# Attention and expert layer in one kernel: the first twelve score tiles in cycles of two slots, and attention products in the gaps between score tiles

## The chip, the cores and the metric

One core of one Trainium2 chip runs the whole program. The metric is the device time of one execution in microseconds (us); the time of the kernel before is the median of three runs.

## The reference

Attention with a threshold, and then a feed-forward layer with a hard-swish gate on its output. There are 8 batches, 8 heads, 576 rows and a head dimension of 64.

```python
scores = scale * np.matmul(q, k.transpose(0, 1, 3, 2))
thresh = np.max(scores, axis=-1, keepdims=True) - tau
scores = np.where(scores >= thresh, scores, -1000000000.0)
attn = np.exp(scores - np.max(scores, axis=-1, keepdims=True))
attn = attn / (np.sum(attn, axis=-1, keepdims=True) + 1e-09)
x = matmul(attn, v), with the heads side by side    # 4608 x 512
h = x @ w_in                                        # 512 -> 2048
out = (h * np.clip(h + 3.0, 0.0, 6.0) / 6.0) @ w_out
```

## The kernel before

**Slots.** The attention is cut into 144 slots (`queue`, lines 188 to 195), 18 for each batch. A slot is 128 rows of q for two heads, so it has two score tiles of 128x576. On every slot the same steps run, each on its own engine:

- TensorE (PE) multiplies q by k into PSUM, in float32, with a contraction of 32 rows at a time. `scores` (line 233) does one slot; `burst` (line 208) does two slots, an even one and the odd one after it, interleaved, so that four groups of 32 rows of the array are in use instead of two.
- VectorE (DVE) copies each tile out of PSUM and takes its row maximum on the way: `sm_max`, line 265, two instructions per slot. `sm_recip` (line 287) later inverts the row sums.
- GpSimd (POOL) makes a bias from the maximum (line 274) and later scales the tile into bf16 (`sm_norm`, line 292).
- ScalarE (ACT) applies the threshold (`sm_mask`, line 279) and the exponential (`sm_exp`, line 284).
- The scaled tile is transposed, by a DMA issued from SyncE (line 303) or, for the slots marked `on_chip`, by PE and a DVE copy (`pe_transpose`, lines 305 to 310).
- PE multiplies the transposed tiles by v (`av`, line 317); DVE copies the product into `xT` (`av_main`, line 325) or `xR` (`av_rest`, line 334). Below these are called **products**.

**The expert layer.** When the four products of a batch and chunk are there, eight items of the first expert matmul are put on the list `todo1` (`whole`, line 408), and four more for every two batches (`odd_items`). Each slot from slot 11 on takes one item: `mm1`, then a relu on ACT (odd slots, line 358) or DVE (even slots, line 360), then the gate on DVE (line 373). Parts of the second expert matmul (`mm2_part`) are done two at a time in odd slots (`second`, line 486). What is left when the 144 slots are done is worked off in a tail (`rest1`, `rest2`, `last_tile`).

**PSUM.** It has eight banks of 512 float32 columns. `score_col` (line 201) puts the score tiles of an even slot at columns 896 to 1472 (banks 1 and 2) and those of an odd slot at 64 to 640 (banks 0 and 1); the second tile of each lies three banks further (banks 4 and 5, and 3 and 4). Bank 1, and bank 4, is thus shared by an even and an odd slot. Banks 6 and 7 (`HB`, `OB`) serve the expert matmuls, the PE transposes and, ahead of slot 11, the products. From slot 11 on the products go to `bank()` (line 178), which is the start of bank 2 or bank 5 in turn, that is, a place in the even slot's own banks.

**Order.** The order of each engine is written by hand: the loop at line 497 emits, for slot n, the maxima of slot n+1, the reciprocal of slot n-1, waiting copies, scores of slot n+2 (while n is at most N1 = 11), the products, an mm1 item, PE transposes, mm2 parts, the exponentials of slot n, the thresholds of slot n+1, transposes of q and k (`jobs`), the scaling of slot n-1, and from slot 12 on, in even slots, the burst of slots n+2 and n+3. Every engine works its list off strictly in that order; what one engine needs of another is a semaphore wait that the recording layer adds. `products`, `jobs`, `issues` and `v_pieces` (lines 420 to 473) say in which slot each product, transpose and load stands.

Of the kernel before, what the change touches and what calls it, by code (L numbers as in the profile page):

```python
# [15 lines left out]
P = 128  # L16
# [4 lines left out]
def kernel(  # L21
# [10 lines left out]
    nc = tc.nc  # L32
# [3 lines left out]
    NPAIR = H // 2  # L36
    KI = d_model // P
    NI = d_ff // P
    NSLOT = 18
    N1 = 11  # L40
    HB, OB = 6, 7
    R, T = 32, S // 32
    scale = 1.0 / math.sqrt(D)
# [24 lines left out]
    qkT = {}  # L68
# [7 lines left out]
    def at(when, n, job):  # L76
        when.setdefault(n, []).append(job)
# [70 lines left out]
                            in_=moe_w_out.rearrange("(ni p) f -> p ni f", p=P)[:, 4 * i:4 * i + 4, :])  # L148

    load(0, 1, 0, 10, by=nc.scalar)  # L150
    load(0, 0, 0, 4)
    load(0, 1, 10, T, by=nc.scalar)
    load(1, 1, by=nc.scalar)
    load(0, 0, 4, T)
    load(1, 0)

    identf = singles.tile([P, P], F32)
# [1 line left out]

    def warm_up(count):  # L160
        for _ in range(count):
            nc.tensor.transpose(ps[:, HB, 0:P], identf[:], identf[:])

    blank = nc.const_aps.tensor(0.0, [P, P], F32)
    for _ in range(2):
        nc.tensor.matmul(ps[:, HB, 0:P], blank, blank, start=True, stop=True)
    warm_up(24)
    identb = singles.tile([P, P], BF16)
    nc.vector.tensor_copy(out=identb[:], in_=identf[:])
# [8 lines left out]
    def bank():  # L178
        nonlocal turn
        turn += 1  # L180
        return ps[:, (2, 5)[turn % 2], :]

    class Slot:
        pass
# [4 lines left out]
    for b in range(B):  # L189
        for g, t in ((0, 0), (0, 1), (1, 0), (1, 1), (None, 4), (0, 2), (0, 3), (1, 2), (1, 3)):  # L190
            for i in range(2):
                sl = Slot()
                sl.b, sl.g, sl.t, sl.i, sl.n = b, g, t, i, len(queue)
                sl.on_chip = sl.n in (1, 3, 5, 6, 7, 8)
                queue.append(sl)


# [3 lines left out]
    def score_col(n, a):  # L201
        return (512 - OWN if n % 2 else 1024 - P) + 1536 * a
# [5 lines left out]
    def burst(n):  # L208
        steps = ((0, 0, P, 0), (1, 0, OWN, 0), (0, 0, P, 1), None,
                 (0, P, OWN, 0), (1, 0, OWN, 1), (0, P, OWN, 1), (1, OWN, P, 0), (1, OWN, P, 1))  # L210
        for step in steps:
# [6 lines left out]
            for a in range(2):  # L218
                c = 32 * (2 * i + a)
                c0 = score_col(n + i, a) + k0  # L220
                for quad, rows, q0 in (((2 * sl.b + sl.g, slice(0, P), sl.t * P),) if sl.t < 4 else
# [4 lines left out]
                                          kT[c:c + 32, j, k0:k0 + w], start=(j == 0), stop=(j == 1))  # L226
                    if (i, k0) == (1, OWN):
                        behind(mm, relay)


    gate = [None]

    def scores(n):
        sl = queue[n]
        quads = [(2 * sl.b + sl.g, slice(0, P), sl.t * P)] if sl.t < 4 else [
            (2 * sl.b + g, slice(64 * g, 64 * g + 64), 512) for g in range(2)]
        own = (P, OWN) if n % 2 == 0 else (0, OWN)
        shared = (0, P) if n % 2 == 0 else (OWN, P)
        for k0, w in (own, shared):
            for j in range(2):  # L240
                for a in range(2):
                    c = 32 * (2 * (n % 2) + a)
                    c0 = score_col(n, a) + k0
                    for quad, rows, q0 in quads:
                        qT, kT = qkT[quad]
                        mm = nc.tensor.matmul(ps_flat[rows, c0:c0 + w],  # L246
                                              qT[c:c + 32, j, q0:q0 + rows.stop - rows.start],
                                              kT[c:c + 32, j, k0:k0 + w], start=(j == 0), stop=(j == 1))
                        if (k0, w) == shared and gate[0] is not None:
                            behind(mm, gate[0])  # L250
        sl.last_mm = mm

    def pass_on(n):
        gate[0] = nc.vector.nop()
        behind(gate[0], queue[n].last_mm)

    def sm_max(sl):
        sl.s = s_pool.tile([P, 2, S], F32, tag="s", name="s")
# [61 lines left out]
    def av_main(b, hp, chunk):  # L320
        if hp == chunk == 0:
            xT[b] = x_pool.tile([P, KI, 512], BF16, tag="xT", name="xT")
        pb = ps[:, OB, P:P + 256] if now < N1 else bank()[:, 0:256]
        av(pb, b, hp, pts[b, hp, chunk], slice(0, 256))
        nc.vector.tensor_copy(out=xT[b][:, hp, 256 * chunk:256 * chunk + 256], in_=pb)  # L325

    def av_rest(b):
        pb = bank()
        for hp in range(NPAIR):
            av(pb[:, 64 * hp:64 * hp + 64], b, hp, ptr[b, hp % 2], slice(64 * (hp // 2), 64 * (hp // 2) + 64))  # L330
        if b % 2 == 0:
            xR[b // 2] = x_pool.tile([P, KI, P], BF16, tag="xR", name="xR")
        o0 = 64 * (b % 2)
        nc.vector.tensor_copy(out=xR[b // 2][:, :, o0:o0 + 64],
                              in_=pb[:, 0:256].rearrange("p (a b) -> p a b", a=NPAIR))

    def half_columns(out, lhsT, rhs, start, stop):
        w = 64 if now < len(queue) - 1 else P
# [82 lines left out]
    for b in range(B):  # L421
        n0 = b * NSLOT
        for hp in range(NPAIR):
            at(products, n0 + 6 + 2 * hp if b else (6, 7, 9, 10)[hp], (b, hp, 0))
            at(products, n0 + 16 + 2 * hp, (b, hp, 1))
        at(products, n0 + 14, (b, None, None))

    def multiply(n):
        for b, hp, chunk in products.get(n, ()):
            if hp is None:  # L430
                av_rest(b)
                if b % 2:
                    todo1.extend(odd_items(b, (0,) if b < B - 1 else (0, 1)))
                elif b:
                    todo1.extend(odd_items(b - 1, (1,)))
            else:
                av_main(b, hp, chunk)
                if hp == NPAIR - 1:
                    todo1.extend(whole(b, chunk))


    for quad in range(2, 2 * B):
        b, g = divmod(quad, 2)
        n0 = (b - 1) * NSLOT
        when = (((6, 7), (9, 10))[g] if b == 1 else ((-2, -1), (6, 7))[g])
        for n, of in zip(when, (1, 0)):
            at(issues, n0 + n, lambda quad=quad, of=of: load(quad, of))
        when = (7, 9, 11, 13) if quad == 2 else ((4, 6, 8, 10), (12, 14, 16, 18))[g]
# [3 lines left out]
    for n, job in ((0, lambda: transpose_k(1, 0)), (0, lambda: transpose_k(1, 1)), (1, lambda: transpose_q(1, 0, 8)),  # L452
                   (2, lambda: transpose_q(0, 8, T)), (4, lambda: transpose_q(1, 8, T))):
        at(jobs, n, job)

# [8 lines left out]
        for i, n in enumerate(slots):  # L464
            at(issues, n, lambda i=i: piece(i))

    v_pieces(0, (0, 0, 1, 1, 2, 2, 3, 3))
    for b in range(1, B):
        v_pieces(b, (16, 17, 18, 19, 20, 21, 22, 23) if b == 1 else [(b - 1) * NSLOT + n for n in range(6, 22, 2)])
    for i, n in enumerate((4, 5, 7, 9)):  # L470
        at(issues, n, lambda i=i: load_w_in(i))
    for i, n in enumerate((11, 13, 15, 17)):
        at(issues, n, lambda i=i: load_w_out(i))

    transpose_k(0, 0)
    transpose_k(0, 1)
    transpose_q(0, 0, 4)
    scores(0)
    pass_on(0)
    sm_max(queue[0])  # L480
    scores(1)
    transpose_q(0, 4, 8)
    for i in range(2):
        sm_mask(queue[0], i)

# [4 lines left out]
            bb, mt, part = todo2.pop(0)  # L490
            mm2_part(mt, part)

    prev = None
    pieces = bb = mt = part = 0
    waiting = []
    outs = []
    for n, sl in enumerate(queue):
        now = n
        if n <= N1:
            pass_on(n + 1)  # L500
        if n + 1 < len(queue):
            sm_max(queue[n + 1])
        if prev is not None:
            sm_recip(prev)
        for copy in waiting:
            copy()
        waiting = []
        if n <= N1:
            scores(n + 2)
        multiply(n)  # L510
        item = None
        if todo1 and n >= N1:
            item, then = todo1.pop(0)
            h = mm1(item, 0 if n == len(queue) - 1 else OB if n > N1 and n % 2 == 0 and not pieces else HB)
# [5 lines left out]
        if n > 1 and queue[n - 2].on_chip:  # L520
            waiting.append(pe_transpose(queue[n - 2]))
# [11 lines left out]
        if prev is not None:  # L533
            sm_norm(prev)
        if n > N1 and n % 2 == 0 and n + 2 < len(queue):
            burst(n + 2)
        if n < 2:
            warm_up(6)
        flush()
        for issue in issues.get(n, ()):  # L540
            issue()
        prev = sl

    for tile in outs:
        late.extend(mm2_out(*tile, on_act=False))
# [11 lines left out]
            by.dma_start(out=out[r0:r0 + P, columns], in_=osb[:, 0:c])  # L557

    def rest1(item, then, on_act=True):
        h = mm1(item, hb=(0, 1, 3, 4)[count[0] % 4])  # L560
        count[0] += 1
        mm1_gate(item, h, mm1_relu(h, on_act))
        todo2.extend(then)
# [12 lines left out]
                late.extend(mm2_out(bb, mt, on_act=(count[1] % 2 == 0)))  # L576
                count[1] += 1

    sm_recip(prev)
    sm_norm(prev)  # L580
    for item in todo1:
        rest1(*item)
    todo1.clear()
    rest2()
    for n in range(len(queue), len(queue) + 5):
        multiply(n)
    for item in todo1:
        rest1(*item)
    rest2()
# [35 lines left out]
```

## Time and profile before

| | us |
|---|---|
| median of 3 runs (lowest, highest) | 558.24 (557.84, 560.10) |
| the profiled execution | 558.5 |
| its span, first to last instruction | 556.7 |
| outside the span | 1.8 |
| PE busy in the span | 524.0 (94%) |
| DVE, ACT, POOL busy | 445.2, 441.8, 280.8 |
| mean granted TensorE clock | 0.926 |
| end of the maxima of slot 13 | 82.8 |

The page of a profile gives the busy time of each engine, then the span in 40 slices of 13.9 us in which each digit is a share in tenths: of busy time, and for PEclk of the full TensorE clock. A busy PE is not a PE at its peak: at half clock the same matmuls are simply busy for longer. The timeline lists instructions in order of time, with start and length in us, merged where equal ones follow each other; in square brackets stands the idle time of the engine ahead of them and who ended it. The view by stretches gives for each stretch the busy time of PE, PE weight loads, DVE, ACT and POOL, and then the granted clock, the share of the DMA engines and GB/s.

### The profile page before, as it was taken

The numbers are of one execution on the slowest core, as the hardware profiler recorded it, in microseconds if no ns is written. First come the engines' busy times: TensorE is split into PE (matmuls) and PEld (weight loads), VectorE is DVE, ScalarE is ACT, GpSimd is POOL, SyncE is SP. The second block draws the span as 40 slices with busy tenths as digits, with TensorE's granted clock in tenths as the row PEclk, the third lists the DMA queues.
The fourth block names the chain that finished last, engine by engine and source line by source line (L and its number), as shares of the span: only waits on it lengthen the run. The fifth ranks groups of instructions, "written<-read, shape, count | busy, mean of one in ns | idle before, by whom it ended". The sixth has DMA issues, their size and how long they took to land.

```text
span 556.7 us, 17228 instructions
## 1 busy us (share of the span) xinstructions
PE 524.0 (94%) x6758; PEld 375.5 (67%) x6758; DVE 445.2 (80%) x1142; ACT 441.8 (79%) x947; POOL 280.8 (50%) x512
## 2 busy tenths in 40 slices
PE   7999996887899999999999999999999999999997
PEld 5655555665677777767776777677767777677555
DVE  3643548766999999989998999899999999898533
ACT  0655438765989898989898989988998989898713
POOL 0354326644655565656555656555565655455300
PEclk8555559988999999999999999999999999999999
DMA  8249577994969898999999999979699977766631
GB/s 170 44 72 163 110 123 112 190 188 100 180 116 199 142 202 133 170 169 175 148 182 185 166 151 167 191 143 192 120 221 159 182 120 125 139 119 107 124 94 40
DMA packets 231154, 81.16 MB, mean 146 GB/s; under 512 B 211872, under 2 KB 224416, under 8 KB 231072
## 3 DMA queue, kind: packets, MB, share of 16 engines
q1 hardware_dynamic: 217056, 69.82, 72.1%
q0 software_dynamic: 13440, 8.92, 13.2%
q10 hardware_dynamic: 576, 1.31, 0.7%
q8 instruction: 53, 0.87, 0.7%
q14 instruction: 29, 0.24, 0.1%
HBM read 36.70 MB, written 9.44 MB: 83 GB/s over the span
## 4 chain that ended last, share of the span: by engine, by line
PE 77%; DVE 13%; DMA 4%; issue 2%; ACT 2%; POOL 0%; SPq 0%; DVEq 0%; POOLq 0%
PE ps L340 36%; PE ps L224 23%; PE ps L246 10%; DVE s L265 6%; PE ps L317 6%; DMA pT<-pn 3%; DVE g L373 3%; ACT r L358 2%; DVE xT L325 1%; PE ps L309 1%; DMA nq<-in_q_dram 1%; DVE r L360 1%; DVE go L373 1%; PE ps L553 1%; DMA nk<-in_k_dram 1%
## 5 line engine op out<-in xcount | busy, mean ns | idle before, releaser
L279 ACT ACTIVATE s<-s,bias 128x576 f32<-128x576 f32 x288 | 205.8, 763 | 37.1 <-POOL bias L274 36.9
L265 DVE TENSOR_SCALAR_CACHE_REDUCE s<-ps 128x576 f32<-128x576 f32 x288 | 205.2, 749 | 35.8 <-PE ps L246 20.7
L292 POOL TENSOR_SCALAR pn<-s,rinv 128x576 bf16<-128x576 f32 x288 | 210.9, 745 | 15.7 <-issue 1.4
L284 ACT ACTIVATE s<-s 128x576 f32<-128x576 f32 x288 | 192.4, 671 | 0.0
L224 PE MATMUL ps<-kT,qT 32*128 32x128 f32 (+3 forms) x2304 | 148.4, 417 | 2.8 <-DVE s L265 2.8
L340 PE MATMUL ps<-xT,w_in_sb 128*64 128x256 bf16 (+1 forms) x1960 | 139.5, 279 | 9.4 <-DVE xT L325 9.3
L224 PEld LDWEIGHTS ps<-kT,qT 32*128 32x128 f32 (+1 forms) x2304 | 110.5, 176 | 42.4 <-issue 7.7
L340 PE MATMUL ps<-w_out_sb,g 128*64 128x512 bf16 (+1 forms) x1040 | 131.7, 380 | 1.1 <-DVE osb L392 1.1
L274 POOL TENSOR_SCALAR bias<-m 128x2 f32<-128x2 f32 (+1 forms) x146 | 27.6, 189 | 206.6 <-DVE rinv L287 190.0
L340 PEld LDWEIGHTS <-w_in_sb 128*64 128x64 bf16 (+1 forms) x1960 | 109.0, 111 | 21.5 <-issue 13.7
L358 ACT ACTIVATE r<-ps,three 128x512 f32<-128x512 f32 x79 | 54.3, 687 | 59.5 <-PE ps L340 53.3
L373 DVE SCALAR_TENSOR_TENSOR g<-r,ps 128x512 bf16<-128x512 f32 x128 | 87.3, 682 | 13.9 <-ACT r L358 10.3
L340 PEld LDWEIGHTS <-g 128*64 128x64 bf16 (+1 forms) x1040 | 62.0, 109 | 49.2 <-issue 2.1
L317 PEld LDWEIGHTS <-v 128*64 128x64 bf16 x960 | 42.8, 114 | 29.6 <-issue 15.5
L317 PE MATMUL ps<-pT,v 128*64 128x256 bf16 x640 | 49.3, 287 | 12.2 <-DMA pT<-pn 4.5
L246 PE MATMUL ps<-kT,qT 32*128 32x448 f32 (+3 forms) x256 | 54.6, 698 | 2.6 <-DVE qT L104 2.6
L360 DVE TENSOR_SCALAR r<-ps 128x512 f32<-128x512 f32 x65 | 44.6, 687 | 14.5 <-PE ps L340 14.0
L284 ACT ACTIVATION_READ_ACCUMULATOR s<-s 128x1 f32 x288 | 54.7, 190 | 0.0
L246 PEld LDWEIGHTS ps<-kT,qT 32*128 32x128 f32 (+1 forms) x256 | 29.7, 296 | 26.8 <-issue 20.0
L126 POOL DMA_DIRECT2D v<-in_v_dram x64 | 36.7, 574 | 19.0 <-PE ps L224 14.9
L325 DVE CAST xT<-ps 128x256 bf16<-128x256 f32 x64 | 26.0, 406 | 22.8 <-PE ps L317 22.7
L392 DVE TENSOR_SCALAR osb<-ps 128x512 f32<-128x512 f32 x32 | 21.8, 683 | 7.0 <-PE ps L340 7.0
(33 smaller groups left out, 195.2 us busy)
## 6 DMA issues: line engine op xcount, KB each, us to landing
nq<-in_q_dram SPq DMA_DIRECT2D x60, 144.0 KB, 4.7
nk<-in_k_dram SPq DMA_DIRECT2D x14, 576.0 KB, 6.0
out_dram<-osb SPq DMA_DIRECT2D x31, 256.0 KB, 3.4
v<-in_v_dram POOLq DMA_DIRECT2D x32, 80.0 KB, 3.3
v<-in_v_dram POOLq DMA_DIRECT2D x32, 64.0 KB, 3.6
w_in_sb<-in_moe_w_in_dram POOLq DMA_DIRECT2D x4, 512.0 KB, 6.5
w_out_sb<-in_moe_w_out_dram POOLq DMA_DIRECT2D x4, 512.0 KB, 7.5
pT<-pn SPq DMA_TRANSPOSE x123, 4.0
```

The costliest lines, as they stand in the source:

```text
L126: nc.gpsimd.dma_start(out=vsb[b % 2][32 * g:32 * g + 32].rearrange("p (hp a) c -> p a hp c", a=2)[:, a, :, c0 * D:(c0 + count) * D], in_=v ...
L224: mm = nc.tensor.matmul(ps_flat[rows, c0:c0 + w], qT[c:c + 32, j, q0:q0 + rows.stop - rows.start], kT[c:c + 32, j, k0:k0 + w], start=(j == ...
L246: mm = nc.tensor.matmul(ps_flat[rows, c0:c0 + w], qT[c:c + 32, j, q0:q0 + rows.stop - rows.start], kT[c:c + 32, j, k0:k0 + w], start=(j == ...
L265: nc.vector.tensor_scalar(out=sl.s[:, i, :], in0=ps_flat[:, c0:c0 + S], scalar1=1.0, scalar2=None, op0=Alu.mult, op1=Alu.max, accum_out=sl ...
L279: nc.scalar.activation(out=s, in_=s, func=Act.Prelu, bias=sl.bias[:, i:i + 1], scale=scale, alpha=REJECT)
L284: nc.scalar.activation(out=s, in_=s, func=Act.Exp, accum_out=sl.rsum[:, i:i + 1])
L292: nc.gpsimd.tensor_scalar(out=pn[:, i, :], in0=sl.s[:, i, :], scalar1=sl.rinv[:, i:i + 1], scalar2=1.0, op0=Alu.mult, op1=Alu.mult)
L317: nc.tensor.matmul(pb[a * 64:(a + 1) * 64, :], vsb[b % 2][:, 2 * hp + a, u * D:(u + 1) * D], pT[:, block, cols], start=(c == 0), stop=(c = ...
L340: nc.tensor.matmul(out[c:c + w], lhsT[:, c:c + w], rhs, start=start, stop=stop)
L358: nc.scalar.activation(out=r, in_=hps, func=Act.Relu, bias=three[:])
L360: nc.vector.tensor_scalar(out=r, in0=hps, scalar1=3.0, scalar2=0.0, op0=Alu.add, op1=Alu.max)
L373: nc.vector.scalar_tensor_tensor(out=out, in0=r, scalar=6.0, in1=hps, op0=Alu.min, op1=Alu.mult)
```

## The change

- The loop over slots 0 to 11 is now a loop over six cycles of two slots. A cycle at n emits: the burst of slots n+2 and n+3, the reciprocals of the last two slots, waiting copies, transposes of q and k, the scaling of the last two slots, the loads of both slots, the four maxima of slots n+2 and n+3, PE transposes, the products of both slots, four idle transposes (`warm_up(4)`), and then exponentials and thresholds. `scores` and its gate are gone. N1 is 12, so the first mm1 item comes one slot later.
- All products go to gaps between score tiles: `bank()` is now columns 640 to 896 (bank 1), or 2176 to 2432 (bank 4), in turn.
- The copies of the products are returned and emitted by the caller: in the cycles one cycle later, in the later slots at once.
- In the later slots the mm1 item is taken from the list ahead of the products of its slot.
- The first load of q has eight row blocks instead of four; loads of v, k, q and the weights stand in other slots; the slots transposed on PE are 0, 2, 4 and 7; the last products of batch 0 come one slot later. In the tail the mm1 items use banks 0, 3, 2, 5 instead of 0, 1, 3, 4.

```diff
-    N1 = 11
+    N1 = 12
...
-    load(0, 0, 0, 4)
+    load(0, 0, 0, 8)
...
-        return ps[:, (2, 5)[turn % 2], :]
+        c0 = P + 512 + 1536 * (turn % 2)
+        return ps_flat[:, c0:c0 + 256]
...
-                sl.on_chip = sl.n in (1, 3, 5, 6, 7, 8)
+                sl.on_chip = sl.n in (0, 2, 4, 7)
...
-        pb = ps[:, OB, P:P + 256] if now < N1 else bank()[:, 0:256]
+        pb = bank()
         av(pb, b, hp, pts[b, hp, chunk], slice(0, 256))
-        nc.vector.tensor_copy(out=xT[b][:, hp, 256 * chunk:256 * chunk + 256], in_=pb)
+        return lambda: nc.vector.tensor_copy(out=xT[b][:, hp, 256 * chunk:256 * chunk + 256], in_=pb)
...
-            at(products, n0 + 6 + 2 * hp if b else (6, 7, 9, 10)[hp], (b, hp, 0))
-            at(products, n0 + 16 + 2 * hp, (b, hp, 1))
-        at(products, n0 + 14, (b, None, None))
+            at(products, n0 + 6 + 2 * hp if b else (6, 7, 10, 11)[hp], (b, hp, 0))
+            at(products, n0 + 16 + 2 * hp + (b == 0), (b, hp, 1))
+        at(products, n0 + 14 + (b == 0), (b, None, None))
...
-    v_pieces(0, (0, 0, 1, 1, 2, 2, 3, 3))
+    v_pieces(0, (0, 0, 2, 2, 2, 4, 4, 4))
...
-    for i, n in enumerate((4, 5, 7, 9)):
+    for i, n in enumerate((6, 6, 8, 8)):
         at(issues, n, lambda i=i: load_w_in(i))
...
-    scores(0)
-    pass_on(0)
-    sm_max(queue[0])
-    scores(1)
+    burst(0)
     transpose_q(0, 4, 8)
+    for i in range(2):
+        sm_max(queue[i])
...
+    for n in range(0, N1, 2):
+        now = n
+        last = [queue[m] for m in (n - 2, n - 1) if m >= 0]
+        burst(n + 2)
+        for sl in last:
+            sm_recip(sl)
+        for copy in waiting:
+            copy()
+        for job in jobs.get(n, ()):
+            job()
+        for sl in last:
+            sm_norm(sl)
+        for issue in issues.get(n, []) + issues.get(n + 1, []):
+            issue()
+        for m in (n + 2, n + 3):
+            sm_max(queue[m])
+        waiting = [pe_transpose(sl) for sl in last if sl.on_chip]
+        waiting += multiply(n) + multiply(n + 1)
+        warm_up(4)
+        for m in (n, n + 1):
+            for i in range(2):
+                sm_exp(queue[m], i)
+            for i in range(2):
+                sm_mask(queue[m + 1], i)
+
+    for n, sl in enumerate(queue[N1:], N1):
+        now = n
+        last = queue[n - 1 - (n == N1):n]
+        if N1 + 1 < n + 1 < len(queue):
             sm_max(queue[n + 1])
...
-        if n <= N1:
-            scores(n + 2)
-        multiply(n)
-        item = None
-        if todo1 and n >= N1:
-            item, then = todo1.pop(0)
+        item = todo1.pop(0) if todo1 else None
+        for copy in multiply(n):
+            copy()
+        if item:
+            item, then = item
...
-        if n > N1 and n % 2 == 0 and n + 2 < len(queue):
+        if n % 2 == 0 and n + 2 < len(queue):
             burst(n + 2)
...
-        h = mm1(item, hb=(0, 1, 3, 4)[count[0] % 4])
+        h = mm1(item, hb=(0, 3, 2, 5)[count[0] % 4])
```

More of the change, by code (lines that the diff above doesn't have):

```diff
@@ L150 @@
     load(0, 1, 0, 10, by=nc.scalar)
-    load(0, 0, 0, 4)
+    load(0, 0, 0, 8)
     load(0, 1, 10, T, by=nc.scalar)
     load(1, 1, by=nc.scalar)
-    load(0, 0, 4, T)
+    load(0, 0, 8, T)
     load(1, 0)
@@ L161, in warm_up @@
         for _ in range(count):
-            nc.tensor.transpose(ps[:, HB, 0:P], identf[:], identf[:])
+            nc.tensor.transpose(ps[:, OB, P:2 * P], identf[:], identf[:])
     blank = nc.const_aps.tensor(0.0, [P, P], F32)
     for _ in range(2):
-        nc.tensor.matmul(ps[:, HB, 0:P], blank, blank, start=True, stop=True)
+        nc.tensor.matmul(ps[:, OB, P:2 * P], blank, blank, start=True, stop=True)
     warm_up(24)
@@ L228, in burst @@
                         behind(mm, relay)
[L231 to L255, printed above, removed]
     def sm_max(sl):
@@ L333, in av_rest @@
         o0 = 64 * (b % 2)
-        nc.vector.tensor_copy(out=xR[b // 2][:, :, o0:o0 + 64],
-                              in_=pb[:, 0:256].rearrange("p (a b) -> p a b", a=NPAIR))
+        return lambda: nc.vector.tensor_copy(out=xR[b // 2][:, :, o0:o0 + 64],
+                                             in_=pb.rearrange("p (a b) -> p a b", a=NPAIR))
     def half_columns(out, lhsT, rhs, start, stop):
@@ L423 @@
         for hp in range(NPAIR):
-            at(products, n0 + 6 + 2 * hp if b else (6, 7, 9, 10)[hp], (b, hp, 0))
-            at(products, n0 + 16 + 2 * hp, (b, hp, 1))
-        at(products, n0 + 14, (b, None, None))
+            at(products, n0 + 6 + 2 * hp if b else (6, 7, 10, 11)[hp], (b, hp, 0))
+            at(products, n0 + 16 + 2 * hp + (b == 0), (b, hp, 1))
+        at(products, n0 + 14 + (b == 0), (b, None, None))
     def multiply(n):
+        copies = []
         for b, hp, chunk in products.get(n, ()):
             if hp is None:
-                av_rest(b)
+                copies.append(av_rest(b))
                 if b % 2:
@@ L436, in multiply @@
             else:
-                av_main(b, hp, chunk)
+                copies.append(av_main(b, hp, chunk))
                 if hp == NPAIR - 1:
                     todo1.extend(whole(b, chunk))
+        return copies
     for quad in range(2, 2 * B):
@@ L444 @@
         n0 = (b - 1) * NSLOT
-        when = (((6, 7), (9, 10))[g] if b == 1 else ((-2, -1), (6, 7))[g])
+        when = (((4, 5), (8, 10))[g] if b == 1 else ((-2, -1), (6, 7))[g])
         for n, of in zip(when, (1, 0)):
             at(issues, n0 + n, lambda quad=quad, of=of: load(quad, of))
-        when = (7, 9, 11, 13) if quad == 2 else ((4, 6, 8, 10), (12, 14, 16, 18))[g]
+        when = (8, 10, 12, 14) if quad == 2 else ((4, 6, 8, 10), (12, 14, 16, 18))[g]
         for n, job in zip(when, (lambda quad=quad: transpose_k(quad, 0), lambda quad=quad: transpose_k(quad, 1),
@@ L451 @@
             at(jobs, n0 + n, job)
-    for n, job in ((0, lambda: transpose_k(1, 0)), (0, lambda: transpose_k(1, 1)), (1, lambda: transpose_q(1, 0, 8)),
+    for n, job in ((0, lambda: transpose_k(1, 0)), (0, lambda: transpose_k(1, 1)), (0, lambda: transpose_q(1, 0, 8)),
                    (2, lambda: transpose_q(0, 8, T)), (4, lambda: transpose_q(1, 8, T))):
@@ L465, in v_pieces @@
             at(issues, n, lambda i=i: piece(i))
-    v_pieces(0, (0, 0, 1, 1, 2, 2, 3, 3))
+    v_pieces(0, (0, 0, 2, 2, 2, 4, 4, 4))
     for b in range(1, B):
-        v_pieces(b, (16, 17, 18, 19, 20, 21, 22, 23) if b == 1 else [(b - 1) * NSLOT + n for n in range(6, 22, 2)])
-    for i, n in enumerate((4, 5, 7, 9)):
+        v_pieces(b, (12, 14, 14, 16, 16, 18, 18, 19) if b == 1 else [(b - 1) * NSLOT + n for n in range(6, 22, 2)])
+    for i, n in enumerate((6, 6, 8, 8)):
         at(issues, n, lambda i=i: load_w_in(i))
-    for i, n in enumerate((11, 13, 15, 17)):
+    for i, n in enumerate((10, 13, 15, 17)):
         at(issues, n, lambda i=i: load_w_out(i))
@@ L491, in second @@
             mm2_part(mt, part)
-    prev = None
     pieces = bb = mt = part = 0
@@ L496 @@
     outs = []
-    for n, sl in enumerate(queue):
+    for n in range(0, N1, 2):
         now = n
-        if n <= N1:
-            pass_on(n + 1)
-        if n + 1 < len(queue):
+        last = [queue[m] for m in (n - 2, n - 1) if m >= 0]
[24 more added lines that the diff above has]
+        if N1 + 1 < n + 1 < len(queue):
             sm_max(queue[n + 1])
-        if prev is not None:
+        for prev in last:
             sm_recip(prev)
@@ L507 @@
         waiting = []
-        if n <= N1:
-            scores(n + 2)
-        multiply(n)
-        item = None
-        if todo1 and n >= N1:
-            item, then = todo1.pop(0)
-            h = mm1(item, 0 if n == len(queue) - 1 else OB if n > N1 and n % 2 == 0 and not pieces else HB)
+        item = todo1.pop(0) if todo1 else None
[3 more added lines that the diff above has]
+            item, then = item
+            h = mm1(item, 0 if n == len(queue) - 1 else OB if n % 2 == 0 and not pieces else HB)
             todo2.extend(then)
@@ L519 @@
         outs = []
-        if n > 1 and queue[n - 2].on_chip:
-            waiting.append(pe_transpose(queue[n - 2]))
         second()
@@ L532 @@
             job()
-        if prev is not None:
+        for prev in last:
             sm_norm(prev)
-        if n > N1 and n % 2 == 0 and n + 2 < len(queue):
+        if n % 2 == 0 and n + 2 < len(queue):
             burst(n + 2)
-        if n < 2:
-            warm_up(6)
         flush()
@@ L541 @@
             issue()
-        prev = sl
     for tile in outs:
@@ L577, in rest2 @@
                 count[1] += 1
-    sm_recip(prev)
-    sm_norm(prev)
+    sm_recip(queue[-1])
+    sm_norm(queue[-1])
     for item in todo1:
@@ L585 @@
     for n in range(len(queue), len(queue) + 5):
-        multiply(n)
+        for copy in multiply(n):
+            copy()
     for item in todo1:
```

## The prediction

> **What bounds the kernel now.** First the page, for which engine and which stage:
>
> ```profile
> PE   7999996887899999999999999999999999999997
> PEclk8555559988999999999999999999999999999999
> ```
>
> PE is busy everywhere, but in slices 2 to 6 (14 to 83 us) it was granted half its clock. The view by stretches has that stage and the later one beside each other (PE, weight loads, DVE, ACT, POOL, clock, DMA):
>
> ```profile
> 13.25:81.50 68.25, 67.81 (x380) 40.63 (x374) 31.63 (x88) 34.06 (x74) 27.05 (x50) 0.50 0.62 102
> 146.40:500.00 353.60, 343.76 (x5158) 254.00 (x5152) 330.40 (x855) 326.50 (x707) 204.58 (x371) 1.00 0.97 161
> ```
>
> In the lead-in PE is the only full engine and slow. Afterwards PE is busy 97%, DVE 93%, ACT 92%. So there are two stages with two prices: **the lead-in (12 slots, ends near 82.8) and the steady stage (from about slot 24 on)**. The timeline shows what a slot costs in the lead-in:
>
> ```profile
> 21.00 4.21 PE L246 MATMUL ps<-kT,qT 32*128 32x448 f32 x16
> 25.14 1.54 PE L162 MATMUL ps<-identf 128*128 128x128 f32 x6
> 25.41 0.76 DVE L265 TENSOR_SCALAR_CACHE_REDUCE s<-ps 128x576 f32<-128x576 f32 x1 [3.48 <-PE ps L246]
> ```
>
> One slot's scores take 4.21 us and DVE waits for them. The maxima of slot 13 end at 82.8, so the first 14 slots have cost (82.8 - 9.35)/14 = 5.2 us each. In the steady stage two slots take 6.51 (burst to burst, mean of 54 pairs from 158.3 to 509.7). Here is one pair:
>
> ```profile
> 225.07 1.06 PE L340 MATMUL ps<-xT,w_in_sb 128*64 128x256 bf16 x16
> 225.97 1.89 PE L340 MATMUL ps<-w_out_sb,g 128*64 128x512 bf16 x16
> 227.70 0.71 PE L317 MATMUL ps<-pT,v 128*64 128x256 bf16 x10
> 228.24 1.04 PE L340 MATMUL ps<-xT,w_in_sb 128*64 128x256 bf16 x16
> 229.21 2.23 PE L224 MATMUL ps<-kT,qT 32*128 32x128 f32 x32
> ```
>
> A burst ended at 225.14; PE then works without a gap through an odd slot's mm1 and mm2, the product of slot 54 (227.70), mm1 and the next burst. DVE meanwhile reads the maxima of slot 55:
>
> ```profile
> 227.51 0.75 DVE L265 TENSOR_SCALAR_CACHE_REDUCE s<-ps 128x576 f32<-128x576 f32 x1
> 228.18 0.08 DVE L265 DVE_READ_ACCUMULATOR s<-ps 128x1 f32 x1
> 228.18 0.75 DVE L265 TENSOR_SCALAR_CACHE_REDUCE s<-ps 128x576 f32<-128x576 f32 x1
> 228.86 0.08 DVE L265 DVE_READ_ACCUMULATOR s<-ps 128x1 f32 x1
> ```
>
> The reader is to see that **the product starts 0.5 us before slot 55's first tile is read, and 1.2 us before that read of both tiles ends**. That overlap is what the change touches.
>
> **Part 1: the lead-in.** It removes 12 runs of `scores` (4.21 each at half clock) and puts six bursts of two slots there. A full-clock burst is 2.23 (above). A half-clock one and the read after it are in the trace too:
>
> ```profile
> 111.26 3.74 PE L224 MATMUL ps<-kT,qT 32*128 32x128 f32 x32
> 115.18 0.76 DVE L265 TENSOR_SCALAR_CACHE_REDUCE s<-ps 128x576 f32<-128x576 f32 x1 [3.40 <-PE ps L224]
> ```
>
> Of that one the first 1.0 us was at full clock, so I take 4.3 for a wholly slow burst. The four maxima after it ran from 115.18 to 118.04: 2.86. A burst waits for the maxima before it (0.06 later) and the maxima for its end (0.18 later). So a cycle is at least 4.3 + 0.18 + 2.86 + 0.06 = **7.4 slow, 5.3 fast**. At full clock POOL is late instead: the maxima of slot n+3 write where slot n-1 is still being scaled, four scalings of 0.745 (3.0) start only behind the burst's relay on POOL (about 1.0), and two maxima (1.4) follow: 5.7 with lags. ACT needs 5.3 a pair and stays below. POOL's list (3.0 + two biases 0.4 + up to three loads of 0.55) is 5.0, plus the relay's wait, and fits.
>
> Which clock? The rows speak for both. Between 13.25 and 81.5 PE counts as busy for 67.81 of 68.25 us and stays at 0.50, so two row groups at work do not raise it; but in 112.2 to 115.7 2.7 us of a four-group burst with the start of mm2 did. And at 92.97 PE was idle for 2.9 us, and the clock fell at 95.2. A cycle has both, a dense 5 us and an idle 2 to 3. I take 6.9, nearer to slow. The Trainium skill ("TensorE: Matmul & The Clock Gate", Part 1) has one busy window of about 3.4 us raise the clock: by it most cycles would be fast, 5.7, and the sum below 7 us less; the 68 busy but slow us show that a busy row is not yet such a window.
>
> Beside the cycles: the larger first q load delays the start (row block two before: 131 KB, at the 165 GB/s seen from 6 to 12 us 0.8; between 0 and 0.8, I take 0.65), so the first burst starts at 9.35 + 0.65 = 10.0 and its maxima end at 10.0 + 4.3 + 0.18 + 2.86 = 17.3. In cycle 6 the two products wait for the maxima (part 2) and, with four idle transposes, stand between them and the next burst: 2 x 0.65 + 0.5 = 1.8 fast, 3.4 slow, 2.6 taken. In cycle 8 their copies (2 x 0.41) wait for the burst and, with the k transposes (0.89), precede the maxima: 1.7. Behind the last cycle stand two products, four transposes and one mm1 ahead of burst 14: 2.8 to 5.2, 4.0 taken. Burst 14 then starts at 17.3 + 6 x 6.9 + 2.6 + 1.7 + 4.0 = 67.0 (fast 57.8, slow 72), against 82.82: **-15.8 (-25 to -11)**. Two more slots go by DMA transpose, and the weight loads are squeezed into 25 us less; I bound that in the next term.
>
> **Part 2: slots 14 to 25.** Products of batch 0 now stand in odd slots and wait for the even slot's maxima ahead of mm1, relu, gate and the odd maxima; pairs 15 to 19 come to some 8 us each, the others to 6 to 8, 44.6 from burst 14 to 26. Before it was 49.5 (82.82 to 132.29), with stalls on DMA (3.2 for pT, 2.5 for v) which earlier v loads and later products relieve, while denser loads may bring others. -5 to +6; I take **-2**.
>
> **Part 3: the steady stage.** The gap is in bank 1 or 4, and these hold part of every score tile. Does PE wait for a reader of other columns of its bank? The trace shows that it does:
>
> ```profile
> 82.14 0.48 PE L224 MATMUL ps<-kT,qT 32*128 32x128 f32 x2 [1.08 <-DVE s L265]
> 82.82 2.22 PE L224 MATMUL ps<-kT,qT 32*128 32x128 f32 x30 [0.20 <-DVE s L265]
> ```
>
> The first two matmuls write columns 896 to 1024 for slot 14. DVE was reading slot 13 at 64 to 640: no column in common, bank 1 in common, and PE idled 1.08 us until the tile was read. The waits recorded in the changed program agree: the product of even slot n waits for the maximum of slot n+1, its first tile in every other pair (bank 1), its second in the others (bank 4). Before, it waited for slot n alone, read long ago. Behind the product on PE stand mm1 and the burst, and for the burst wait all maxima, so the period grows by the whole wait. In the pair shown the tiles are read at 228.26 and 228.93; with 0.06 lag the product starts 0.62 or 1.29 later than 227.70, mean 0.96. From slot 26 to 142 there are 59 such products: 59 x 0.96 = 56. What goes: mm1 waited for xT behind its own product,
>
> ```profile
> PE ps L340 <- DVE xT L325: 9.1, 13, 0.9
> ```
>
> and as the item is now taken first, those 9.1 us vanish. **+47 (40 to 54**, DVE's small work moves the maxima by up to 0.3 either way). The burst's new wait for the copy of the product costs nothing: the copy (0.40) runs under mm1 (1.04).
>
> The Trainium skill ("PSUM — Partial Sum Buffer", PSUM bank collisions raise a hardware error) speaks against the change in the same way: guard PSUM by bank, not by address. If waits went by address, part 3 would be -9 instead of +47, and the sum 535.
>
> **Part 4: the tail.** First items come one slot later and chunk 1 of batch 0 two: two mm1 items (0.93 each there: 64 matmuls in 7.40) and one pair of mm2 parts (1.89) move to the tail: **+3.7 (1 to 5)**. Its other banks cost nothing: they are free by then.
>
> **Sum**, on the profiled execution: 556.7 - 15.8 - 2 + 47 + 3.7 = 589.6, and 1.8 outside the span: 591.4. That execution (558.5) stands 0.3 above the median, so **591** against 558.24.
>
> **Rivals.**
> - *The waits are hidden* (faster). If DVE came to the odd maxima 1.3 us earlier relative to PE, products would find the bank free. Place: the steady pair; price 0; it turns at a net 0.24 us a pair ((15.8 + 2 - 3.7)/59), against 0.80 ((56 - 9.1)/59). Time 558.2 - 15.8 - 2 - 9.1 + 3.7 = 535. Against it: the gate (0.69) stands between the two maxima in DVE's order, and is not moved. 0.08.
> - *The lead-in doesn't get shorter*: bursts always slow, POOL and DMA late, cycles near 10 us, so part 1 is worth 0: 607. For it: loads squeezed together; against: no row of 10 us. 0.12.
> - *The clock falls in the steady stage too*, as PE now idles once a pair. A slow stretch lasts 3.4 us and loses half of it; one in every two pairs (14.6 us), over 400 us, is 27 x 1.7 = 46: 637. Against: 115.7 to 119.1 held 1.4 us of idle time and kept the clock. 0.08.
> - *As forecast*: 0.72, by its own bounds (-25 - 5 + 40 + 1, -11 + 6 + 54 + 5) 569 to 612.
>
> The range **570 to 612** takes in the forecast with its bounds and the second rival, and leaves out the others. Half a per cent is about what a measurement of this kernel can tell from no change: faster 0.08, within 0.5% 0.02, slower 0.90.
>
> **What would show it.** Lead-in: maxima of slot 13 near 63 and burst 14 near 67, bursts of four groups from 10 us on. Steady: PE idle ahead of products, released by DVE's maxima, some 0.6 and 1.3 in turn, 50 to 60 us in all; periods of 6.9 and 7.6 in place of 6.5; no more wait for xT ahead of mm1; PE busy 85 to 90% there at clock 1.00. Wrong, if products start without that wait, or if burst 14 starts after 80.

## The result, and the profile after

The changed kernel takes **596.78 us** (median of 4 runs, 593.40 to 599.56), against 558.84 (557.84 to 560.10) for the kernel before in the same comparison. The ratio is 1.068, with a 95% interval of 1.061 to 1.074. Executions over 1.5% longer than the fastest one of the same kernel are left out of every ratio in this document, on both sides, so a ratio can differ a little from the quotient of the medians. The profiled execution took 597.0, its span 595.1, at a mean granted clock of 0.962 (before: 556.7 and 0.926).

First the two lines of the page that were shown for the kernel before, here with the share of each engine in the chain that ended last and that chain by line:

```profile
PE   5765877878888788888888888888888888888997
PEclk8888777998999999999999999999999999999999
...
PE 51%; DVE 33%; ACT 5%; issue 3%; POOL 1%; DMA 1%; DVEq 0%; POOLq 0%
PE ps L314 22%; DVE s L239 19%; PE ps L225 18%; PE ps L291 10%; DVE g L347 7%; ACT r L332 4%; DVE r L334 2%; DVE osb L366 2%; DMA v<-in_v_dram 1%; POOL pn L266 1%; DVE kT L118 1%; DVE go L347 1%; PE ps L546 1%; DVE qT L104 1%; DVE rinv L261 0%
```

The clock of the lead-in rose from 5 tenths to 7 or 8, as the bursts of four groups were to bring about. But PE, nines from end to end before, is now an eight in nearly all of the later stage, and a third of the last chain is VectorE. In the view of waits PE's largest item says for what (waiting engine and line, releaser, us in total, times, longest):

```profile
PE ps L291 <- DVE s L239: 69.2, 66, 4.0
PE ps L225 <- DVE s L239: 13.1, 17, 2.3
PE ps L225 <- DVE qT L104: 4.2, 1, 4.2
PE ps L283 <- POOL pn L266: 1.9, 4, 1.0
```

L291 is the matmul of `av`, a product; L239 is `sm_max`, the maxima. The wait for xT is gone. Two stretches of the view by stretches, the lead-in and the steady one (PE, weight loads, DVE, ACT, POOL, clock, DMA share, GB/s):

```profile
13.25:58.00 44.75, 28.40 (x300) 21.81 (x301) 27.47 (x79) 32.62 (x72) 24.70 (x47) 0.84 0.75 122
...
146.40:500.00 353.60, 310.36 (x4531) 225.08 (x4532) 301.31 (x759) 287.87 (x624) 183.64 (x331) 1.00 0.88 145
```

In the steady stretch the clock is full and PE is idle for 43.2 of 353.6 us; before it was 9.8. One pair of slots on PE:

```profile
222.92 1.89 PE L314 MATMUL ps<-w_out_sb,g 128*64 128x512 bf16 x16
226.01 0.74 PE L291 MATMUL ps<-pT,v 128*64 128x256 bf16 x10 [1.19 <-DVE s L239]
226.55 1.07 PE L314 MATMUL ps<-xT,w_in_sb 128*64 128x256 bf16 x16
227.55 2.23 PE L225 MATMUL ps<-kT,qT 32*128 32x128 f32 x32
229.71 1.06 PE L314 MATMUL ps<-xT,w_in_sb 128*64 128x256 bf16 x16
230.60 1.89 PE L314 MATMUL ps<-w_out_sb,g 128*64 128x512 bf16 x16
232.95 0.74 PE L291 MATMUL ps<-pT,v 128*64 128x256 bf16 x10 [0.45 <-DVE s L239]
```

Product, mm1, burst, mm1, mm2, product is the same order as before. From the start of mm2 to that of the product it was 1.73 us; here it is 3.09 and 2.35. On DVE, the reads of the odd slot's tile that each of these two products waited for (the second tile ahead of 226.01, the first ahead of 232.95):

```profile
225.19 0.75 DVE L239 TENSOR_SCALAR_CACHE_REDUCE s<-ps 128x576 f32<-128x576 f32 x1
...
232.14 0.75 DVE L239 TENSOR_SCALAR_CACHE_REDUCE s<-ps 128x576 f32<-128x576 f32 x1
```

Each product starts 0.06 or 0.07 us after the end of that read. Why PE can't catch up is told by the chain of waits of the same stretch (start, length, what):

```profile
226.01 0.74 PE ps L291 x10
226.74 0.87 PE ps L314 x16
227.62 2.16 PE ps L225 x28
229.78 1.01 PE ps L314 x16
230.79 0.02 issue
230.81 0.70 ACT r L332
231.51 0.02 issue
231.53 0.69 DVE g L347
232.22 0.69 DVE s L239 x2
232.91 0.04 issue
232.95 0.74 PE ps L291 x10
```

**The chain has become a loop**: product, mm1, burst, the odd slot's mm1, its relu on ACT, its gate on DVE, the first tile's maximum, and the next product, 6.94 us round. Where the product goes to bank 4 the loop holds the second tile too. Before, the products stood outside of this loop.

By stages of the profiled executions (us; "burst 14" is the burst of slots 14 and 15, in the kernel before without its first two matmuls; E1, below, is the changed kernel with its later products in the old banks):

| | before | E1 | after |
|---|---|---|---|
| to the start of burst 14 | 82.8 | 63.1 | 64.7 |
| burst 14 to burst 26 | 49.5 | 47.0 | 50.6 |
| burst 26 to the end of the maxima of slot 143 | 383.5 | 372.0 | 434.9 |
| from there to the end of the span | 41.0 | 43.6 | 44.8 |
| mean pair of slots, 32 to 141 | 6.519 | 6.312 | 7.405 |

### The profile page after: what moved, and what is told of

Read it like the earlier page. It is cut to its first block, busy times and chain, and to the rows that moved or that the text cites. A ratio compares the mean times of both kernels' runs of the same rounds, so it can differ in the third digit from the quotient of the medians.

```text
span 595.1 us, 17141 instructions
## 1 busy us (share of the span) xinstructions
PE 500.6 (84%) x6724; PEld 366.2 (62%) x6728; DVE 453.2 (76%) x1140; ACT 441.5 (74%) x947; POOL 282.6 (47%) x512
## 4 chain that ended last, share of the span: by engine, by line
PE 51%; DVE 33%; ACT 5%; issue 3%; POOL 1%; DMA 1%; DVEq 0%; POOLq 0%
PE ps L314 22%; DVE s L239 19%; PE ps L225 18%; PE ps L291 10%; DVE g L347 7%; ACT r L332 4%; DVE r L334 2%; DVE osb L366 2%; DMA v<-in_v_dram 1%; POOL pn L266 1%; DVE kT L118 1%; DVE go L347 1%; PE ps L546 1%; DVE qT L104 1%; DVE rinv L261 0%
## 5 line engine op out<-in xcount | busy, mean ns | idle before, releaser
L239 DVE TENSOR_SCALAR_CACHE_REDUCE s<-ps 128x576 f32<-128x576 f32 x288 | 205.2, 751 | 32.7 <-PE ps L225 23.1
L225 PE MATMUL ps<-kT,qT 32*128 32x128 f32 (+3 forms) x2560 | 174.5, 431 | 17.4 <-DVE s L239 13.1
L225 PEld LDWEIGHTS ps<-kT,qT 32*128 32x128 f32 (+1 forms) x2560 | 130.9, 182 | 63.7 <-issue 19.0
L314 PE MATMUL ps<-xT,w_in_sb 128*64 128x256 bf16 (+1 forms) x1944 | 137.4, 278 | 0.1
L314 PEld LDWEIGHTS <-w_in_sb 128*64 128x64 bf16 (+1 forms) x1944 | 110.2, 111 | 9.4 <-issue 2.2
L291 PEld LDWEIGHTS <-v 128*64 128x64 bf16 x960 | 45.7, 115 | 95.0 <-issue 88.5
L291 PE MATMUL ps<-pT,v 128*64 128x256 bf16 x640 | 50.5, 285 | 63.0 <-DVE s L239 61.7
L118 DVE STREAM_TRANSPOSE kT<-nk 128x320 f32<-128x320 f32 (+1 forms) x64 | 26.4, 451 | 1.4 <-DMA nk<-in_k_dram 1.4
L104 DVE STREAM_TRANSPOSE qT<-nq 128x640 f32<-128x640 f32 (+2 forms) x33 | 24.6, 749 | 2.5 <-DMA nq<-in_q_dram 2.5
```

Source lines behind the costliest of these rows:

```text
L225: mm = nc.tensor.matmul(ps_flat[rows, c0:c0 + w], qT[c:c + 32, j, q0:q0 + rows.stop - rows.start], kT[c:c + 32, j, k0:k0 + w], start=(j == ...
L239: nc.vector.tensor_scalar(out=sl.s[:, i, :], in0=ps_flat[:, c0:c0 + S], scalar1=1.0, scalar2=None, op0=Alu.mult, op1=Alu.max, accum_out=sl ...
L291: nc.tensor.matmul(pb[a * 64:(a + 1) * 64, :], vsb[b % 2][:, 2 * hp + a, u * D:(u + 1) * D], pT[:, block, cols], start=(c == 0), stop=(c = ...
L314: nc.tensor.matmul(out[c:c + w], lhsT[:, c:c + w], rhs, start=start, stop=stop)
```

## The experiments

The theory: PSUM is guarded by bank, so a product in a gap waits for the maxima of the odd slot, and this costs about 1 us in each of 59 pairs; the lead-in is a gain beside it. The first five runs test that, the others ask how much of the lead-in's gain can be kept. Ratios are to the kernel before, run beside each. Beside the experiments it took from 549.4 to 564.7 us, and in every experiment all executions of the variant lie on one side of all of those of the kernel before in that comparison.

**E1: the later products back in banks 2 and 5**, all else as in the changed kernel.

```diff
-        c0 = P + 512 + 1536 * (turn % 2)
+        c0 = P + 512 + 1536 * (turn % 2) if now < N1 else 512 * (2, 5)[turn % 2]
```

> The changed kernel, but from slot 12 on the products go to banks 2 and 5 again, as in the kernel before; the cycles keep the gaps. My theory (a product in a gap waits for the maxima of the slot after its own, because they read the same bank): the steady pair falls from 7.40 to about 6.35 us (the kernel before has 6.52 and waits 9 us in all for xT, which the new order of items takes away), the waits of products for DVE from slot 26 on fall from some 55 us to under 5, and the time is about 64.7 (burst 14 as in the changed kernel) + 50.6 (to burst 26, where batch 0 still waits in odd slots) + 374 (before: 383.5, less 9.1) + 44.8 (tail) + 1.8 = 536. Rival one (the new order of items, products and copies costs the time, not the bank): about 597, unchanged. Rival two (PE's idle clock or later loads): 570 or more, with waits gone and periods still over 7.

Measured: **530.2 us** (527.6 to 536.6), ratio 0.953 (0.940 to 0.965). The wait and the steady stretch:

```profile
PE ps L291 <- DVE s L239: 13.7, 9, 3.1
...
130.00:460.00 330.00, 328.78 (x4970) 243.97 (x4964) 317.98 (x821) 314.20 (x680) 197.68 (x358) 1.00 1.01 166
```

Of the 66 waits 9 are left, none after 127 us, and PE is again almost without a gap: a pair takes 6.31 us of plain PE work. The time is 6 below the 536 expected; the table shows that the lead-in, slots 14 to 25 and the steady stage all came out shorter than was put. One address made the kernel slower; the rest of the change made it faster.

**E2: the gaps alone, put into the kernel before** (its products from slot 11 on).

```diff
-        return ps[:, (2, 5)[turn % 2], :]
+        c0 = P + 512 + 1536 * (turn % 2)
+        return ps_flat[:, c0:c0 + 256]
```

> The kernel before with one thing changed: bank() is the gap (bank 1 or 4), so products from slot 14 on go there. My theory: the steady pair grows from 6.52 to about 7.4 or a little more, as the wait for xT ahead of mm1 stays, 60 products times 0.8 to 1.0 us: 605 to 620. If the cycles or the order of items were what makes the changed kernel slow: within 1% of 559.

Measured: **620.7 us** (617.2 to 624.5), ratio 1.117 (1.104 to 1.131); a pair takes 7.503 in place of 6.519, and 59 x 0.984 = 58. The wait appears as expected, and the time lies just above the range:

```profile
PE ps L318 <- DVE s L266: 65.8, 64, 3.6
```

**E3: the later products in the gap of bank 1 only**, so that each waits for the first tile and none for the second.

```diff
-        c0 = P + 512 + 1536 * (turn % 2)
+        c0 = P + 512 + (1536 * (turn % 2) if now < N1 else 0)
```

> The changed kernel, but from slot 12 on all products go to the gap in bank 1, none to bank 4. My theory: each product then waits for the first tile of the next slot alone, so all steady pairs have the shorter of the two periods (7.07 and 7.72 in the changed kernel, in turn), some 0.65 us less in 30 pairs: about 577. If the wait were for something else than the read of the tile in the same bank (columns, the copy, a general cost of writing PSUM beside DVE): 597, or slower, as one gap in place of two makes each product wait for the copy of the one before.

Measured: **576.3 us** (572.0 to 580.8), ratio 1.035 (1.021 to 1.048). Pairs take 6.99 and 7.13, where the changed kernel's take 7.07 and 7.72 in turn.

```profile
PE ps L291 <- DVE s L239: 45.9, 66, 3.0
```

As many waits, but without the longer kind. So the price goes by the tile that lies in the bank, and not by the copy of the product or by the gap's being used again at once.

**E7: the mm1 item ahead of the product on PE**, so that other work fills the wait.

```diff
+        if item:
+            h = mm1(...)
         for copy in multiply(n):
             copy()
-        if item:
-            h = mm1(...)
```

> The changed kernel (products in the gaps), with the mm1 item ahead of the product on PE in the later slots. mm1 (1.0 us) then fills the wait for the first tile and most of that for the second. My theory: the waits of products for DVE fall from 55 to some 10 us, but the burst now waits for the copy of the product, which is in its own bank and can't start before the product has ended: a steady pair of about 7.1 in place of 7.40, 59 x 0.3 = 18 us less, 578. If PE's idle time ahead of the product were the whole loss: 6.4 a pair and 540.

Measured: **575.1 us** (572.4 to 576.5), ratio 1.034 (1.025 to 1.044), a pair 7.13.

```profile
PE ps L291 <- DVE s L239: 21.7, 38, 3.0
PE ps L225 <- DVE xT L299: 14.1, 29, 0.5
```

The wait falls by 47.5, but a new one comes: now the burst stands right behind the product and waits for its copy. Only part of the loss is hidden in this order. Of the 0.8 us a pair that E7 still takes more than E1, 0.4 lies between the start of the product and that of the burst, and 0.1 ahead of the product; the burst itself is 0.3 longer, which was not explained.

**E8: in the kernel before, only the mm1 item taken ahead of the products** (the part of the change that prices the xT wait).

```diff
-        multiply(n)
         item = None
         if todo1 and n >= N1:
             item, then = todo1.pop(0)
+        multiply(n)
+        if item:
             h = mm1(...)
```

> The kernel before, with the mm1 item taken from the list ahead of the products of its slot, as the change has it, and nothing else. This is the term of 9.1 us of my sum by itself: mm1 no longer waits for xT behind its own product (9.3 us in all go), and one item and one pair of mm2 parts more go to the tail. 549 to 553, against 559. If another wait takes the place of that for xT: within 0.5% of 559.

Measured: **541.3 us** (539.3 to 549.8), ratio 0.973 (0.962 to 0.984), a larger gain than expected. The profiled execution is the longest, 549.8 (the others: 539.3 to 542.6), so only its steady stage is read here: a pair takes 6.327 in place of 6.519, 59 x 0.192 = 11.3 us. The prediction had 9.1 for the xT wait. From the start of mm1 to that of the burst behind it, where this wait lay, the time fell from 1.21 to 0.97 us in the regular pairs (mm2, product, mm1, burst), which covers the 11.3. What the other executions gained beyond that was not traced.

**E4: E1, and in the lead-in the products in banks 7 and 6**, which hold no scores, with their copies in the same cycle. It is to take away the 3.96 us for which the changed kernel's products of slots 10 and 11 waited for maxima:

```profile
59.55 2.35 PE L291 MATMUL ps<-pT,v 128*64 128x256 bf16 x20 [3.96 <-DVE s L239]
```

```diff
-        pb = bank()
+        pb = bank() if now >= N1 else ps[:, HB, 0:256] if hp == 3 else ps[:, OB, 256:512]
...
-            at(products, n0 + 6 + 2 * hp if b else (6, 7, 10, 11)[hp], (b, hp, 0))
+            at(products, n0 + 6 + 2 * hp if b else (6, 8, 10, 11)[hp], (b, hp, 0))
...
-        waiting += multiply(n) + multiply(n + 1)
         warm_up(4)
+        for copy in multiply(n) + multiply(n + 1):
+            copy()
```

> As the first run, and in the cycles the four products go to banks 6 and 7, which no score tile uses, with their copies in the same cycle, the idle transposes ahead of them, and the second product one cycle later. My theory: the products then run under the maxima instead of behind them; the cycles with products lose some 5 us (cycle 6) and 3 us (the last) and the copies no longer hold up cycle 8 (0.8): about 8 us less than the first run, 528, with burst 14 near 57. Rival (the cycles wait for loads of v and weights, not for the bank): burst 14 stays at 62 to 65 and the time is that of the first run within 3 us.

Measured: **533.0 us** (532.1 to 533.6), ratio 0.959 (0.947 to 0.970). The expectation failed: burst 14 came at 67.3, 4 us later than in E1. Here is the product of slots 10 and 11:

```profile
63.26 2.34 PE L291 MATMUL ps<-pT,v 128*64 128x256 bf16 x20 [8.90 <-DMA pT<-pn]
```

The bank was free, but the transposed tile was not there yet: behind the wait for the bank stood a wait for a transfer.

**E5: E4 with the expert weights loaded later.**

```diff
-    for i, n in enumerate((6, 6, 8, 8)):
+    for i, n in enumerate((6, 8, 12, 14)):
         at(issues, n, lambda i=i: load_w_in(i))
-    for i, n in enumerate((10, 13, 15, 17)):
+    for i, n in enumerate((15, 16, 17, 18)):
```

> The fourth run again, with the loads of the weights spread over later slots (w_in at 6, 8, 12, 14 and w_out at 15 to 18, instead of 6, 6, 8, 8 and 10 to 17). The fourth run lost 8.9 us where the product of slot 10 waited for a DMA transpose. If that transpose was late because the weight loads kept the DMA engines busy: the wait falls under 3 us, burst 14 starts near 60 in place of 67.3, and the time is 525 to 529. If it was late because of its own queue or of the scaling before it: still 6 us or more, and 532.

Measured: **530.4 us** (527.2 to 532.1), ratio 0.954 (0.942 to 0.966). Burst 14 came at 55.3, 12 us before E4's, and the wait of 8.90 for the transpose is down to 0.56:

```profile
51.54 1.28 PE L291 MATMUL ps<-pT,v 128*64 128x256 bf16 x20 [0.56 <-DMA pT<-pn]
```

So it was the weights' loads that had delayed the transposes there. But burst 26 came at 111.9, later than E1's 110.2: the gain was given back in slots 14 to 25.

**E6: E1 with twelve idle transposes a cycle in place of four.**

```diff
-        warm_up(4)
+        warm_up(12)
```

> The first run with 12 idle transposes in each cycle in place of 4. If the clock falls in the cycles because PE idles 2 to 3 us in them, the filler holds it up: six cycles near 5.7 in place of 6.0 to 7.1, the granted clock from 15 to 60 us near 1.0, burst 14 near 60 (63.1 in the first run), time 526 to 528. If idle transposes don't count as work for the clock: the clock flips as before, and where it is at half the 2.6 us of filler delay the next burst: burst 14 at 64 to 67.

Measured: **530.1 us** (528.1 to 531.7), ratio 0.954 (0.945 to 0.962). The same stretch of the lead-in, E1 first and then E6:

```profile
20.70:41.20 20.50, 14.70 (x166) 11.22 (x166) 13.65 (x41) 16.31 (x36) 14.22 (x26) 0.82 0.56 99
```

```profile
20.70:41.20 20.50, 14.42 (x190) 11.21 (x188) 14.24 (x44) 17.17 (x38) 14.92 (x28) 1.00 0.57 97
```

The clock was held in this stretch, and from burst 4 to burst 8 it bought 0.3 us (11.4 against 11.7); burst 14 came no earlier (63.6 against 63.1). One reason can be read from the waits of DVE from 10 to 64 us: the maxima wait 7.0 us for the scaling on POOL (E1: 7.2), and this a faster PE doesn't shorten. Over 10 to 63 us the clock rose only from 0.74 to 0.84, less than was expected, so what a full clock all through would bring is not shown.

**E9 and E10: the products of batch 0's second chunk and rest back in even slots**, E9 on E5 and E10 on E1.

```diff
-            at(products, n0 + 16 + 2 * hp + (b == 0), (b, hp, 1))
-        at(products, n0 + 14 + (b == 0), (b, None, None))
+            at(products, n0 + 16 + 2 * hp, (b, hp, 1))
+        at(products, n0 + 14, (b, None, None))
```

> e5_weights_later with one more edit: the products of the first batch's second chunk and of its rest stand in even slots again (n0 + 16 + 2 * hp and n0 + 14 for both batches), in banks 2 and 5. In e5 burst 14 began at 55.3 us, but the 13 pairs to burst 26's were then long (7.7 to 10.5) and burst 26 began at 111.9. Theory: the products that stand in odd slots there hold mm1, and with it the chain of relu, gate and the odd slot's maxima, by 1.0 to 1.7 us each plus their own length on TensorE; in even slots the second tile's bank has long been read, and the pairs of slots 14 to 25 fall towards 7. Then burst 14 stays near 55, burst 26 begins near 100 to 104 and the time is 519 to 523 us. Rival: the stretch is full, of TensorE work at a clock between 0.5 and 1 and of VectorE's copies of the products, or late transposes of the probabilities take the place of the wait; then burst 26 stays at 110 to 112 and the time at 528 to 532.

> e1_old_banks_later with the same edit, the weights' loads left where they are. In e1 burst 14 began at 63.1 us and burst 26 at 110.2 (47.1 for 12 slots). Theory: as above, by less, since these slots were shorter: burst 14 near 63, burst 26 near 105 to 108, time 525 to 528 us. Rival: no change, 530 within its run to run spread.

Measured: E9 **528.0 us** (523.9 to 531.5), ratio 0.956 (0.945 to 0.967); E10 **526.4 us** (525.8 to 530.8), ratio 0.956 (0.947 to 0.965). Burst 26 began at 113.2 and 113.9, so the theory failed in both, and the rival held: E10's time lies in the range that the theory gave, but burst 26 doesn't come earlier in its trace. Two limits of these traces: E10's profiled execution is the longest of its six, 4.3 us above the median; and E9, which up to slot 13 is E5's code, had burst 14 at 60.5 where E5 had it at 55.3, so the lead-in can differ by 5 us between executions. E10's longest wait, and the times from issue to landing of the transposes that were issued between 66 and 86 us (least, median, most):

```profile
83.21 1.28 PE L291 MATMUL ps<-pT,v 128*64 128x256 bf16 x10 [7.27 <-DMA pT<-pn]
```

```profile
DMA to landing us min/median/max: 7.0/7.9/10.3
```

**E11 and E12: loads left out.** This asks whether transfers bound slots 14 to 25.

```diff
     nc.vector.memset(three[:], 3.0)
+    nc.vector.memset(w_out_sb[:], 0.0)
...
-    for i, n in enumerate((10, 13, 15, 17)):
-        at(issues, n, lambda i=i: load_w_out(i))
```

> e10_odd_products_back with the second expert matrix never loaded: VectorE sets its place to zero before the first scores, so the output is zero, and 2.1 MB of loads in slots 10 to 17 are gone (every matmul is still done). In e10 the stretch from burst 14 to burst 26 took 50.2 us, in which PE was busy 36.3, the busy share of the DMA engines was 1.21 at 171 GB/s, and transposes landed 7 to 10 us after their issue. Theory: that stretch is bounded by transfers, loads and transposes together; 2.1 MB at 171 GB/s are 12 us. Then burst 26 comes 8 to 12 us earlier (102 to 106 in place of 113.9), the waits of products for transposes (11.0 us) fall under 4, and the time is 515 to 520 us. Rival: the waits for the maxima and the clock hold the stretch; then burst 26 moves by less than 3 us.

> e11 with the first expert matrix not loaded either (GpSimd sets it to zero before the first scores), another 2.1 MB of loads gone, in slots 6 to 8. Theory: burst 14 comes earlier too, by the part of the wait of the products of slots 10 and 11 that transposes cause, but this wait in e10 is mostly for a PSUM bank (about 3 us for the maxima), so burst 14 moves by 0 to 4 us, and burst 26 comes to 97 to 104: time 510 to 517 us. Rival as for e11: burst 26 within 3 us of e10's.

Measured: E11 **518.2 us** (517.2 to 519.3), ratio 0.931 (0.925 to 0.937); E12 **518.4 us** (517.5 to 519.3), ratio 0.932 (0.925 to 0.939). In E11 burst 14 began at 64.3 and burst 26 at 100.9: 36.6 us in place of E10's 50.2. In medians the gain is smaller, 8.2 us, as E10's profiled execution is a long one. The transposes issued between 66 and 86 us land in little over half the time,

```profile
DMA to landing us min/median/max: 3.2/4.3/4.7
```

and the waits of products for them fall from 11.0 to 1.3. With the waits gone the clock of the stretch rose too, from 0.86 to 1.00. **So transfers, with the loads of w_out among them, bound slots 14 to 25 in E10**; that they also took back E5's gain is likely, but not tested. E12 adds nothing (burst 26 at 100.0) and misses the 510 to 517 expected: without w_out's loads, w_in's are no limit.

## Why the prediction was right, point by point

- **Part 3, the steady stage: right in mechanism, too small by 4.5.** Predicted +47, measured +51.5 (burst 26 to the maxima of slot 143). The waits in turn were put at 0.62 and 1.29; in the pair shown the product is later, counted from mm2's start, by 0.62 and 1.36. Two terms were mis-sized. The 59 products cost 434.9 - 372.0 = 62.9 (the changed kernel against E1) and not 56, that is 7.405 - 6.312 = 1.09 a pair of slots and not 0.96. In the 47 pairs of slots 32 to 141 that have the order shown, the product starts 1.01 later than in E1, and the product and the mm1 behind it take 0.05 longer; two pairs without an mm2 ahead of the product lose 1.85 each. The other way, the end of the xT wait was worth more than 9.1: E1 is 383.5 - 372.0 = 11.5 shorter than the kernel before, and E8's pairs give 11.3.
- **Part 1, the lead-in: right, -18.1 against -15.8.** The maxima of slots 0 and 1 ended 1.2 earlier than predicted, and the five plain cycles took 6.1 on average in place of 6.9, together 4.0 less. The clock went between 1.0 and 0.5, as was expected from a cycle that has both kinds of row. The cycle behind the first products took 12.9 where 6.9 + 2.6 + 1.7 = 11.2 was put (+1.7; the first of these products waited 1.4 for a load of v, which was not in the sum), and the way from the last cycle to burst 14 took 5.2 in place of 4.0 (+1.2).
- **Part 2, slots 14 to 25: wrong in sign, +1.1 against -2.** The stalls of products on transfers went, as predicted. But the clock in this stretch was 0.83 (before 0.90, E1 0.93), and products waited 7.0 us for maxima. E1, without the gaps from slot 12 on, has 47.0 there, -2.5 against before; so the later products in the gaps cost 3.6 in this stretch. Without them, transfers bound it (E11, for E10).
- **Part 4, the tail: right**, +3.9 against +3.7.
- **The sum**: the span was to grow by 589.6 - 556.7 = 32.9 and grew by 595.1 - 556.7 = 38.4. The 5.5 between them are -2.3 (part 1), +3.1, +4.5 and +0.2. That it came so close is in part luck: in part 1 terms that were 5.2 too high stand against others 2.9 too low, and in part 3 the 6.9 more for the products against 2.4 more for the end of the xT wait.
- **The rivals.** Hidden waits were priced at 535. E1, in which the waits are not there, gives 530. The lead-in did get shorter, so the second rival is out. The turning point stood rightly with the gate between the maxima: it is a piece of the loop in the chain above. The clock was 1.00 in the steady stretch though PE idles once in each pair, so the third rival didn't come about.

The Trainium skill ("PSUM — Partial Sum Buffer", PSUM bank collisions raise a hardware error) has PSUM guarded by bank and not by address; that was the side taken. The waits in this program, which the recording layer adds, go by bank: E1, E2 and E3 show the price of such guards. No run here shows what an overlap without them would do.

**What stays open.** Six variants (E1, E4, E5, E6, E9, E10) have medians of 526 to 533 us and ratios of 0.953 to 0.959 whose intervals overlap. All beat both kernels; which is best was not told apart. Nor was an order of loads found that keeps E5's early burst 14 past slot 25.

## What to carry to other kernels

A free stretch of columns in a PSUM bank is no free place: where waits go by bank, as here, a matmul into it waits for the readers of the other columns too, so choose the bank whose readers finish first in the order of the work, and not the one with room. Ask of a new wait whether what it waits for depends, around some corner, on what stands behind the waiting instruction: then it is a loop, its length is the new period, and no engine's share of busy time shows it (here none is above 88% of the steady stretch). And a gain in one stage can be lost in the next, as E5's was: look there for waits on transfers and for landing times that grow.

## What the runs showed of the hardware that was not expected

- **The clock doesn't follow the busy share.** In the lead-in PE was busy 99% of the time at 0.50 before, and 63% of the time (28.40 of 44.75 us) at 0.84 after. Idle transposes count: with twelve a cycle the clock was 1.00 from 20.7 to 41.2 us, with four 0.82, at much the same busy time (14.4 and 14.7 of 20.5); in the ten profiles of kernels with four a cycle it lay between 0.73 and 0.92 there. The Trainium skill ("TensorE: Matmul & The Clock Gate", Part 4) says that PE transposes don't count as busy in the same way. These float32 ones speak against it, though only one profile has twelve a cycle.
- **A transpose by DMA takes nearly twice as long beside the weights' loads**: 7.9 us from issue to landing (median, 66 to 86 us) in E10, 4.3 in E11, with 2.1 MB of loads less in that stage. Over the whole kernel before the median was 4.0.
